# Two DMA queues for two streams of tiles: V loads issued from ScalarE, K loads from SyncE, in a cached attention decode kernel

## The chip, the cores and the metric

One core of one Trainium2 chip. The metric is the device time of the launch in microseconds (us), the median of several runs. Before the change: 2566.66 us (2565.97 to 2567.49, 3 runs). All runs that are compared are of the fast state, except where a line says otherwise.

Terms: PE is the matrix engine (TensorE), which also forms sums here by multiplying with an identity matrix; VectorE and ScalarE do the elementwise work; SyncE here only issues transfers. SBUF is the memory on the chip that tiles are loaded into. An engine *issues* a load into its own queue, the 16 DMA engines move it in packets, and it has *landed* when its completion records are in. PV is the product of the softmax weights with a V tile. "Page", "timeline" and "windows" are views of the profile of one execution.

## The reference, cut to what matters

```python
# twice, for A and for B; B=8 sequences, one new token each, H=32 heads, Sk=4096 keys, Dh=128, bf16
q = (x @ wq).reshape(B, 1, H, Dh).transpose(0, 2, 1, 3)
scores = einsum("bhqd,bhkd->bhqk", q, k_cache) * Dh ** -0.5
o = einsum("bhqk,bhkd->bhqd", softmax(scores), v_cache)
result = o.transpose(0, 2, 1, 3).reshape(B, 1, H * Dh) @ wo
```

The four caches are 1.07 GB, each byte used once. A decode step is one long read with a little arithmetic beside it.

## The kernel before

The work is cut into 64 steps, `n` (2 problems x 8 sequences x 4 groups of 8 heads). Each step needs one K tile and one V tile of 128 partitions x 64 KB (8.39 MB). The kernel keeps three in SBUF: K tiles alternate between slots 0 and 1, and all V tiles but the last share slot 2. So K is double-buffered and V is not. VectorE multiplies K with q and folds it, in four chunks; PE and VectorE finish the sums; the softmax weights are spread into `PM`; PE computes PV, in two halves.

```python
plan = [("wq", 0, 1), ("k", 0, 0), ("wq", 1, 2)]        # kind, number, slot
for n in range(NQ - 1):
    plan.append(("k", n + 1, (n + 1) % 2))
    plan.append(("v", n, 2))
...
def load_tiles():                       # issue what is next in the plan once its slot is free
    while issued[0] < len(plan):
        kind, n, w = plan[issued[0]]
        prev = before[issued[0]]        # the slot's former tenant
        dep = opUse.get(prev)           # its last reader on PE
        if prev is not None and dep is None:
            return
        to, key = ring[:, w, :], ("t", w)
        if kind in ("k", "v"):
            ...
            opT[(kind, n)] = dma(to, from_, key, [dep])     # SyncE's queue
...
for n in range(NQ):
    for r in range(NR):                 # NR = 4 chunks of a K tile
        make_mul(s)                     # VectorE, L330: waits for K
        if s >= LAG: make_red(s - LAG)  # VectorE, L353: waits for PE's sums of the chunk before
        ...
        fold = make_fold(s)             # VectorE, L335
        ...
        if r == 2 and n >= 1:
            make_pv(n - 1, 0, RG // 2)  # PE, L382: waits for V
        if r == 3 and n >= 1:
            make_pv(n - 1, RG // 2, RG)
            make_acc(n - 1)             # ScalarE: pv -> accS, L390
        if r == 2 and n + 1 < NQ: ...   # q of the next step (make_stage, make_qbc)
        make_eacc(s, fold)              # PE, L345: sums of this chunk; the fourth frees K's slot
        load_tiles()
        if r == 3 and n >= 1: make_ext(n - 1)   # PE, then ScalarE's small output copy
```

Note PE's order: the first half of PV stands ahead of chunk 2's sums. If V is late, PE waits, and VectorE soon waits behind PE.

Of the kernel before, what the change touches and what calls it, by code (L numbers as in the profile page):

```python
# [31 lines left out]
class _Program:  # L32
# [11 lines left out]
    def add(self, eng, emit, deps=(), dma_key=None, moves=False):  # L44
        op = _Op(eng, emit, list(deps), dma_key, moves)
        if dma_key is not None:
            self.counts[dma_key] = self.counts.get(dma_key, 0) + 16
            op.token = (dma_key, self.counts[dma_key])
        for d in op.deps:
            if not (d.eng == "pe" and eng == "pe"):  # L50
                d.sig = True
        self.ops[eng].append(op)
        return op
# [86 lines left out]
def _build_kernel(nc, caches, out):  # L140
    B, Sq, D = caches[0][0].shape
    _, H, Sk, Dh = caches[0][1].shape
    NC = len(caches)
    assert B == 8 and Sq == 1 and Dh == 128 and Sk == 4096 and D == 1024 and H % 8 == 0 and 128 % H == 0
# [7 lines left out]
    HB = H // HQ  # L152
    NQ = NC * HB * B
# [8 lines left out]
    with es:  # L162
# [19 lines left out]
        pe = sb("pe", [128, T], BF16)  # L182
# [17 lines left out]
        sems = {e: es.enter_context(nc.semaphore(f"c_{e}")) for e in ENGINES[1:]}  # L200
# [4 lines left out]
        P = _Program()  # L205
        add = P.add

        def dma(out_ap, in_ap, key, deps, eng="sp"):
            return add(eng, lambda e: e.dma_start(out_ap, in_ap), deps, dma_key=key)
# [21 lines left out]
        opT, opMul, opEacc, opRed, opNgm, opExp = {}, {}, {}, {}, {}, {}  # L231
# [18 lines left out]
        def where(n):  # L250

            return n // (B * HB), n // HB % B, n % HB
# [4 lines left out]
        def load_tiles():  # L257
            while issued[0] < len(plan):
                kind, n, w = plan[issued[0]]
                prev = before[issued[0]]  # L260
                dep = opUse.get(prev)
# [3 lines that stand above are left out]
                if kind in ("k", "v"):  # L265
                    c, b, hb = where(n)
                    from_ = caches[c][1 if kind == "k" else 2][b, hb * HQ:(hb + 1) * HQ].rearrange("u (m t) d -> (u m) (t d)", m=MP)
                    opT[(kind, n)] = dma(to, from_, key, [dep])
                elif kind == "wq":
                    opT[(kind, n)] = dma(to[:, 0:DC * H * Dh], caches[n][3].rearrange("(p k) n -> p (k n)", k=DC), key, [dep])  # L270
                else:
                    from_ = caches[n][4].rearrange("(p r) n -> p (r n)", r=H)
                    for i, (r0, r1) in enumerate(wo_cuts if n == NC - 1 else ((0, H),)):
                        opT[(kind, n, i)] = dma(to[:, r0 * D:r1 * D], from_[:, r0 * D:r1 * D], key if n < NC - 1 else ("w", i), [dep])
                issued[0] += 1
# [171 lines left out]
        def emit_xT(e):  # L447
# [5 lines left out]
            return i  # L453
        op_xT = opUse[("x", 0)] = add("pe", emit_xT, [c_ident, op_x[-1]])
        load_tiles()
        c_xT = add("dve", lambda e: e.tensor_copy(xT[:], misc_bf16[:, 0:NC * DC * B]), [op_xT])
        make_q(0)
# [5 lines left out]
        for n in range(NQ):  # L463
            P.mark(n)
            for r in range(NR):
                s = n * NR + r
                make_mul(s)
                if s >= LAG:
                    make_red(s - LAG)
                if r == LAG - 1 and n >= 1:  # L470
                    make_shift(n - 1)
                fold = make_fold(s)
                if r == LAG - 1 and n >= 1:
                    make_pm(n - 1)
                if n == 0 and r == 1:
                    for c in range(1, NC):
                        make_q(c)
                        make_qT(c)
                if r == 2 and n >= 1:
                    make_pv(n - 1, 0, RG // 2)  # L480
                if r == 3 and n >= 1:
                    make_pv(n - 1, RG // 2, RG)
                    make_acc(n - 1)
                if r == 2 and n + 1 < NQ:
                    make_stage(n + 1)
                    make_qbc(n + 1)
                make_eacc(s, fold)
                load_tiles()
                if r == 3 and n >= 1:
                    make_ext(n - 1)  # L490
        P.mark(NQ)
        n = NQ - 1
# [4 lines left out]
        make_pv(n, 0, RG)  # L497
        make_acc(n)
        load_tiles()
        make_ext(n)  # L500
        make_norm(1)
# [4 lines left out]
        counts = P.tokens()  # L506
        for o in op_x:
            o.token = (("x", 0), 16 * NC)
        loops = {"pe": (1, 2, (NQ - 2) // 2), "dve": (3, 2, (NQ - 4) // 2), "act": (3, HB, (NQ - 4) // HB)}

        @block.sync
        def _(eng):
            P.run("sp", eng, sems)
            eng.wait_ge(sems[("out", 0)], counts[("out", 0)])
# [4 lines left out]

        @block.scalar  # L520
        def _(eng):
            P.run("act", eng, sems, loops["act"])

        @block.vector
        def _(eng):
# [7 lines left out]
def bass_concat_heads__mha_block_cached__mha_block_cached__decode_kernel(  # L533
    nc, A_x, A_k_cache, A_v_cache, A_wq, A_wo, B_x, B_k_cache, B_v_cache, B_wq, B_wo, out,
):
    caches = [(A_x, A_k_cache, A_v_cache, A_wq, A_wo), (B_x, B_k_cache, B_v_cache, B_wq, B_wo)]
    _build_kernel(nc, caches, out)
# [28 lines left out]
```

## Time and profile before

| before | value | where |
|---|---|---|
| DMA engines' busy share, rate, steady state | 1.00, 433 GB/s | windows, 120 to 2400 us |
| bytes read | 1107.33 MB, 2557 us at that rate | page |
| VectorE busy per period of 38.7 us | 33.81 us | windows, 1013.5 to 1052.2 us |
| VectorE's wait for K | 303.4 us in all | page, L330 |

The page of the kernel before: span, busy time, DMA slices (a digit of 9 is 90% or more), the DMA queues (packets, MB, share of the 16 engines' time) and three groups of instructions (busy us, mean ns | idle us before, and what ended most of it): VectorE's L330, which waits for K, its L353, which waits for PE's sums, and PE's PV at L382:

```profile
span 2565.3 us, 18707 instructions
PE 1125.5 (44%) x7648; PEld 395.3 (15%) x7648; DVE 2172.4 (85%) x1043; ACT 130.0 (5%) x401; POOL 2.6 (0%) x14
...
DMA  9999999999999999999999999999999999999998
...
q1 hardware_dynamic: 19344, 1107.32, 99.8%
...
L330 DVE TENSOR_TENSOR ring<-ring,qbc 128x8192 bf16<-128x8192 bf16 x256 | 1131.1, 4418 | 303.4 <-DMA ring<-in_B_k_cache_dram 153.3
...
L353 DVE TENSOR_REDUCE s_sb<-red 128x64 f32<-128x1024 f32 x256 | 311.0, 1215 | 3.7 <-PE red L345 3.7
L382 PE MATMUL pv<-ring,PM 128*32 128x512 bf16 x4096 | 274.0, 415 | 4.6 <-DVE PM L370 4.6
...
ring<-in_A_k_cache_dram SPq DMA_DIRECT2D x32, 40.0
ring<-in_A_v_cache_dram SPq DMA_DIRECT2D x32, 27.9
```

VectorE is busy 85% of the time, but the DMA engines are busy all of it, in one queue. 1107.33 MB at 433 GB/s fill 2557 of the 2565 us: at this rate, by that estimate, no order of the same loads can win more than 0.4%.

The timeline before, cut to the issues, the PV halves and VectorE's starts on K (start us, us, engine, line, operation; in brackets the idle time before):

```profile
1002.91 1.91 PE L382 MATMUL pv<-ring,PM 128*32 128x512 bf16 x32
1004.86 0.33 SPq L209 DMA_DIRECT2D ring<-in_A_v_cache_dram  x1
...
1011.96 0.33 SPq L209 DMA_DIRECT2D ring<-in_A_k_cache_dram  x1
...
1013.51 4.42 DVE L330 TENSOR_TENSOR ring<-ring,qbc 128x8192 bf16<-128x8192 bf16 x1 [4.82 <-DMA ring<-in_A_k_cache_dram]
...
1035.51 1.91 PE L382 MATMUL pv<-ring,PM 128*32 128x512 bf16 x32
...
1041.64 1.91 PE L382 MATMUL pv<-ring,PM 128*32 128x512 bf16 x32
1043.60 0.33 SPq L209 DMA_DIRECT2D ring<-in_A_v_cache_dram  x1
```

Read it as turns. V is issued at 1004.9, as soon as PV has left its slot, but the engines are still on the K tile that VectorE receives at 1013.5. V flows after that, alone, for 19.35 us, and is there (27.9 us after its issue, 1032.8) before PE wants it at 1035.5. From then until its next issue at 1043.6 the V slot takes no data, and the engines spend that time on K. V's **turnaround**, landing to next issue, is hidden under K's turn.

### The profile page before, as it was taken

The page shows a single profiled execution, that of the slowest core. Times are in us where ns is not written, and L with a number is a line of the kernel's source. Part 1 is how long each engine was busy: PE and PEld are TensorE (multiplying, and loading weights), DVE is VectorE, ACT ScalarE, POOL GpSimd, SP SyncE. Part 2 cuts the span into 40 slices and gives each one's busy share as a digit, 9 for nine tenths or more (in the row PEclk, how much of TensorE's full clock was granted, in tenths as well). Part 3 has the DMA queues.
Part 4 walks back from the last instruction along what each step waited for, and adds up shares of the span by engine and source line. Part 5 has one row for each costly group of instructions (what it writes and reads, how often), then busy time and mean ns, then how long its engine had stood idle before and what let it go on. Part 6 is the DMA issues. An engine that isn't in the chain of part 4 may idle for free.

```text
span 2565.3 us, 18707 instructions
## 1 busy us (share of the span) xinstructions
PE 1125.5 (44%) x7648; PEld 395.3 (15%) x7648; DVE 2172.4 (85%) x1043; ACT 130.0 (5%) x401; POOL 2.6 (0%) x14
## 2 busy tenths in 40 slices
PE   2543443444444444444444434444444434434435
PEld 0111111111111111111111111111111111111112
DVE  2898898898898898898888888988988988988983
ACT  1100000000000000000000000000000000000000
POOL 0000000000000000000000000000000000000000
PEclk7666667676766767767766767667766757667677
DMA  9999999999999999999999999999999999999998
GB/s 425 425 425 441 433 433 433 433 435 431 435 431 435 431 435 432 435 431 435 432 435 431 435 431 436 430 436 430 437 429 437 429 437 430 436 431 435 431 436 381
DMA packets 19435, 1107.51 MB, mean 432 GB/s; under 512 B 2209, under 2 KB 2257, under 8 KB 2401
## 3 DMA queue, kind: packets, MB, share of 16 engines
q1 hardware_dynamic: 19344, 1107.32, 99.8%
q8 instruction: 7, 0.11, 0.0%
q10 hardware_dynamic: 80, 0.05, 0.0%
q14 instruction: 4, 0.02, 0.0%
HBM read 1107.33 MB, written 0.03 MB: 432 GB/s over the span
## 4 chain that ended last, share of the span: by engine, by line
DMA 51%; DVE 28%; issue 16%; PE 5%; another core or an unknown queue 0%; ACT 0%; DVEq 0%; SPq 0%
DMA ring<-in_B_k_cache_dram 25%; DMA ring<-in_A_k_cache_dram 25%; DVE ring L330 10%; DVE ring L335 10%; PE red L345 4%; DVE s_sb L353 4%; DVE PM L370 3%; DMA ring<-in_B_wo_dram 1%; DVE rmax L359 1%; DVE rtmp L360 0%; PE proj L433 0%; ACT PM L291 0%; PE o L285 0%; DVEq L135 0%
## 5 line engine op out<-in xcount | busy, mean ns | idle before, releaser
L345 PE MATMUL red<-ring,ident 128*128 128x512 bf16 x2048 | 785.6, 553 | 1380.5 <-DVE ring L335 1380.5
L330 DVE TENSOR_TENSOR ring<-ring,qbc 128x8192 bf16<-128x8192 bf16 x256 | 1131.1, 4418 | 303.4 <-DMA ring<-in_B_k_cache_dram 153.3
L335 DVE TENSOR_TENSOR ring<-ring 128x4096 bf16<-128x4096 bf16 x256 | 581.4, 2271 | 0.0
L345 PEld LDWEIGHTS red<-ring,ident 128*128 128x128 bf16 x2048 | 239.7, 128 | 1833.6 <-DVE ring L335 1482.9
L353 DVE TENSOR_REDUCE s_sb<-red 128x64 f32<-128x1024 f32 x256 | 311.0, 1215 | 3.7 <-PE red L345 3.7
L382 PE MATMUL pv<-ring,PM 128*32 128x512 bf16 x4096 | 274.0, 415 | 4.6 <-DVE PM L370 4.6
L370 DVE TENSOR_TENSOR PM<-pe,own_h 128x2048 bf16<-128x2048 bf16 x64 | 146.1, 2283 | 0.7 <-ACT pe L365 0.7
L382 PEld LDWEIGHTS pv<-ring,PM 128*32 128x32 bf16 x4096 | 103.9, 104 | 189.0 <-issue 116.3
L319 ACT ACTIVATE qbc<-misc 128x128 bf16<-128x128 f32 x64 | 17.8, 278 | 1072.4 <-PE misc L317 1072.4
L365 ACT ACTIVATE pe<-s_sb,ngm 128x256 bf16<-128x256 f32 x64 | 32.5, 508 | 468.5 <-DVE ngm L363 468.5
L390 ACT ACTIVATE accS<-pv 128x512 bf16<-128x512 f32 x64 | 38.2, 597 | 349.0 <-PE pv L382 349.0
L399 PEld LDWEIGHTS o<-accS,E 128*32 128x32 bf16 x1024 | 31.3, 100 | 49.4 <-issue 48.2
L399 PE MATMUL o<-accS,E 128*32 128x32 bf16 x1024 | 38.1, 185 | 0.7 <-ACT accS L390 0.7
L405 ACT ACTIVATE o_sb<-o 32x32 f32 (+1 forms) x64 | 11.9, 186 | 454.4 <-PE o L399 453.8
L305 DVE COPY qT<-misc 128x64 bf16<-128x64 bf16 x8 | 3.5, 435 | 33.3 <-PE misc L301 33.3
L359 DVE TENSOR_REDUCE rmax<-s_sb 128x1 f32<-128x256 f32 x64 | 26.9, 420 | 2.2
L438 DVE CAST orow<-proj 40x512 bf16<-40x512 f32 (+1 forms) x2 | 1.1, 554 | 26.7 <-PE proj L433 26.7
L433 PE MATMUL proj<-ring,on_sb 128*8 128x256 bf16 (+1 forms) x192 | 15.2, 395 | 13.8 <-DMA ring<-in_A_wo_dram 8.7
L312 ACT ACTIVATE qst<-qT 128x128 bf16 (+1 forms) x64 | 18.7, 293 | 2.0 <-DVE qT L305 2.0
L360 DVE TENSOR_SCALAR rtmp<-half,rmax 128x32 f32<-128x32 f32 x64 | 15.4, 241 | 2.2
L285 PE MATMUL o<-ring,xT 128*8 128x512 bf16 x64 | 7.1, 621 | 20.0 <-DMA ring<-in_A_wq_dram 11.0
L363 DVE TRANSPOSE_TENSOR_REDUCE ngm<-rtmp 128x1 f32<-128x32 f32 x64 | 13.5, 211 | 2.2
(33 smaller groups left out, 74.4 us busy)
## 6 DMA issues: line engine op xcount, KB each, us to landing
ring<-in_B_wo_dram SPq DMA_DIRECT2D x1, 6144.0 KB, 35.0
ring<-in_B_wo_dram SPq DMA_DIRECT2D x1, 1536.0 KB, 38.3
ring<-in_A_k_cache_dram SPq DMA_DIRECT2D x32, 40.0
ring<-in_A_v_cache_dram SPq DMA_DIRECT2D x32, 27.9
ring<-in_B_k_cache_dram SPq DMA_DIRECT2D x32, 39.8
ring<-in_B_v_cache_dram SPq DMA_DIRECT2D x32, 27.9
ring<-in_B_wo_dram SPq DMA_DIRECT2D x1, 512.0 KB, 39.0
out_dram<-orow SPq DMA_DIRECT2D x2, 4.0 KB
```

The lines of the kernel that those rows point to most:

```text
L312: return e.activation(qst[:, n % 2, :].rearrange("p (j m) -> p j m", m=MP), from_.unsqueeze(2).to_broadcast([128, HQ, MP]), ACTF.Copy)
L319: opQbc[n] = add("act", lambda e: e.activation(qbc[:, n % 2, :], misc[:, 0:Dh], ACTF.Copy), [opQb[n], _at(opMul, NR * (n - 2) + NR - 1)])
L330: opMul[s] = add("dve", lambda e: e.tensor_tensor(v, v, qbc[:, n % 2, :].unsqueeze(1).to_broadcast([128, CT, Dh]), ALU.mult), [opT[("k", n ...
L335: return add("dve", lambda e: e.tensor_tensor(v[:, :, 0:64], v[:, :, 0:64], v[:, :, 64:128], ALU.add), [opMul[s]])
L345: i = e.matmul(dst, ident[:], v[:, g, :, j, :], start=(j == 0), stop=(j == 3))
L353: opRed[s] = add("dve", lambda e: e.tensor_reduce(s_sb[:, n % 2, r * CT:(r + 1) * CT], red_ps[s % 2][:, :].rearrange("p (t w) -> p t w", w ...
L359: m = add("dve", lambda e: e.tensor_reduce(rmax[:], s_sb[:, n % 2, :], AX.X, ALU.max), [opRed[NR * n + NR - 1]])
L365: opExp[n] = add("act", lambda e, at: e.activation(pe[:], s_sb[:, n % 2, :], ACTF.Exp, bias=ngm[:, n % 2:n % 2 + 1], scale=scale, accum_ou ...
L370: opPM[n] = add("dve", lambda e: e.tensor_tensor(PM[:], pe[:].unsqueeze(2).to_broadcast([128, T, HQ]), own_h[:].unsqueeze(1).to_broadcast( ...
L382: i = e.matmul(pv_ps[32 * q:32 * (q + 1), :], PM[:, t:t + 4, :].rearrange("p t j -> p (t j)"), v[:, t * Dh:(t + 4) * Dh], start=(g == 0), ...
L390: opAcc[n] = add("act", lambda e: e.activation(accS[:], pv_ps[:], ACTF.Copy), [opPV[n], _at(opExt, n - 1)])
L399: x = e.matmul(to, E[:, i, PH - 1 - u:PH - 1 - u + MB], accS[:, i * 128 + H * u:i * 128 + H * (u + 1)], start=(i == 0 and u == 0), stop=(i ...
```

## The change

Its intent: do not hold a V load behind the K load that stands ahead of it in a queue; start it at once on a second queue. ScalarE then issues loads that can't stand in its loop, so its program is written out straight.

```diff
-                    opT[(kind, n)] = dma(to, from_, key, [dep])
+                    opT[(kind, n)] = dma(to, from_, key, [dep], "act" if kind == "v" else "sp")
...
-        loops = {"pe": ..., "dve": ..., "act": (3, HB, (NQ - 4) // HB)}
+        loops = {"pe": ..., "dve": ...}
...
-            P.run("act", eng, sems, loops["act"])
+            P.run("act", eng, sems)
```

More of the change, by code (lines that the diff above doesn't have):

```diff
@@ L508, in _build_kernel @@
             o.token = (("x", 0), 16 * NC)
-        loops = {"pe": (1, 2, (NQ - 2) // 2), "dve": (3, 2, (NQ - 4) // 2), "act": (3, HB, (NQ - 4) // HB)}
+        loops = {"pe": (1, 2, (NQ - 2) // 2), "dve": (3, 2, (NQ - 4) // 2)}
         @block.sync
```

## The prediction

> **What bounds the kernel now.** DMA. The page's slices show the 16 DMA engines 9 tenths busy or more; queue q1 is 99.8% of it. The kernel reads 1107.33 MB; in the steady state (windows view, 120 to 2400 us) the rate is 433 GB/s. All bytes at that rate take 2557 of 2565.3 us: under 0.5% is left to win. VectorE is next: 33.8 us busy per period of 38.7 us (one K and one V tile), with 4.8 us waiting for K (303.4 us in all, L330). One 8.39 MB tile takes 19.35 us.
>
> **Order now.** One queue serves whole tiles in turn. In the timeline V is issued at 1004.9, K at 1012.0, while the former K lands at 1013.5: V waits 8 us for its turn, then flows alone (27.9 us to landing). The 10 us in which PV holds the only V slot are covered by K's turn.
>
> **The change.** V gets a second queue. [...] ScalarE's second x load, 16 KB, issued at 1.4 us beside SyncE's loads, lands at 10.8. So V and K will share the rate half and half. Issue costs (0.3 to 0.6 us on ScalarE, 5% busy) and the straight ScalarE program cost nothing visible.
>
> **As a cycle.** Sharing stretches V, the tile with one slot. Let V land at t=0 with PE blocked on it (PV stands before chunk 2's reduction matmuls in PE's order, so VectorE blocks too):
> - PV half 3.4 [...], qbc 1, reduction 2.2, PV half 1.9, gaps 0.4: slot free at 8.9; accS copy 0.6; issue to first packet about 1: next V flows from 10.3.
> - VectorE: reduce 1.2, fold 2.3 end at 10.0; last reduction matmuls 1.9; next K issued at 12.0, flowing from 13.1.
> - V has 2 to 3 of its 8 packets per DMA engine (2.42 us each) alone, then alternates with K: 13 to 14 packet times, 31.4 to 33.9 us. It lands at 42 to 44.5; K two to three packets later, 5 to 7 us into the next cycle; then DMA idles until 10.3.
>
> VectorE wants V at 33 (22 us after its tile starts at 10.7), so it does wait and the cycle sustains itself. Period 42 to 45 instead of 38.7, all on the critical path: V's turnaround, hidden before. Today's phase leads there: sharing delays K's landing by 8 us, then V's issue. 63 periods of 43.6 plus the 128 us outside them (2565 - 63 x 38.7) give about 2880.
>
> **Prediction: 2880 us**, 8 in 10 within 2720 to 3060. Faster by over 2%: 0.01; within 2%: 0.10; slower by over 2%: 0.89.
>
> **What would show it.** Two queues, about half the bytes each; DMA busy near 0.9, about 385 GB/s; V's issue to landing up from 27.9 to about 33; PE waiting for V at L382 (about 10 us per period), VectorE's wait moving from L330 (K) to L353 (reduction); VectorE's busy time unchanged at 2172 us; period 42 to 45.
>
> **What would make it wrong.** If the DMA engines favour one queue, tiles keep landing one by one and the time stays near 2566. If K joins later or earlier than costed, the period moves by whole packets (2.4 us, 150 us in all). If PE's restart is quicker, the idle shrinks. If the phase locks so that V ends before it is wanted, the time is near the DMA bound again.

63 x 43.6 + 128 comes to 2875, about 2880. Two terms were estimates. Of the half share, the trace before shows only that the second queue is served while the first is busy: the two x loads' packets run from 1.8 to 10.1 us, while SyncE's wq load, issued at 0.81 us, takes 21.9 us to land. PV's 3.4 us has its likeness in the sums of 8 matmuls at L345: 3.60 us at 80.59 us, where TensorE's granted clock was 0.50 of full speed, and 1.90 us at 114.41 us, where it was 1.00.

## The result, and the profile after

After: 2931.91 us median (2924.83 to 2936.99, 3 runs), **14% slower**: ratio 1.1421, 95% interval 1.1401 to 1.1440. (Here and below a ratio is the mean time of one kernel's fast runs over that of the other's fast runs of the same rounds, so not quite the ratio of the medians.) The instructions of PE and VectorE are the same as before, in the same order.

The same lines of the page of the changed kernel, with a second queue:

```profile
span 2935.2 us, 18256 instructions
PE 1155.4 (39%) x7648; PEld 401.4 (14%) x7648; DVE 2172.8 (74%) x1043; ACT 130.0 (4%) x401; POOL 2.5 (0%) x14
...
DMA  9989889889889898898898898898988988988989
...
q1 hardware_dynamic: 10128, 570.45, 44.9%
q10 hardware_dynamic: 9296, 536.92, 43.7%
...
L330 DVE TENSOR_TENSOR ring<-ring,qbc 128x8192 bf16<-128x8192 bf16 x256 | 1131.4, 4420 | 13.6 <-DMA ring<-in_A_k_cache_dram 13.6
...
L353 DVE TENSOR_REDUCE s_sb<-red 128x64 f32<-128x1024 f32 x256 | 312.2, 1220 | 659.8 <-PE red L345 659.8
L382 PE MATMUL pv<-ring,PM 128*32 128x512 bf16 x4096 | 349.5, 502 | 799.9 <-DMA ring<-in_A_v_cache_dram 400.1
...
ring<-in_A_k_cache_dram SPq DMA_DIRECT2D x32, 37.6
ring<-in_A_v_cache_dram ACTq DMA_DIRECT2D x32, 36.3
```

Two queues carry half of the bytes each. The DMA engines are now busy 44.9 + 43.7 = 88.6% of the span instead of 99.8%. VectorE works as long as before, hardly waits for K (13.6 us) and waits 659.8 us behind PE, which waits 799.9 us for V. V takes 36.3 us from issue to landing instead of 27.9, although it is now first in its queue.

The chain of waits of the changed kernel between 1490 and 1560 us (start us, us, what):

```profile
1504.83 36.34 DMA ring<-in_B_v_cache_dram
1541.17 0.04 issue
1541.21 3.61 PE pv L382 x32
1544.82 0.22 PE misc L317
1545.04 2.28 PE red L345 x8
1547.32 1.87 PE pv L382 x32
1549.19 0.02 issue
1549.21 0.01 ACT accS L390
1549.21 38.88 DMA ring<-in_B_v_cache_dram
```

This is the whole period: V flows 36.34 us, PE needs 8.04 us to use it up, then the next V is issued; 1504.83 to 1549.21 is 44.38 us, against 38.7 before. The next one takes 38.88 us, one packet more. K appears nowhere: its issue lies beside this chain, as the timeline cut to SyncE (1490 to 1512 us) shows:

```profile
1508.38 0.33 SPq L209 DMA_DIRECT2D ring<-in_B_k_cache_dram  x1
```

So K joins 3.55 us after V. Each time the V slot is turned around, K has already ended: in the trace's packet records of this period the last K packet ends at 1545.6 and the next V packet starts at 1550.2. The 4.6 us between are idle on all 16 engines; 62 such stretches between the first tiles and the last sum to 293 us of the 370 us by which the span grew. Of the rest, 39 us is longer packets (their time per engine sums to 2600 us instead of 2561 us), and what is left, by subtraction, is time in which only some of the 16 are idle.

### The profile page after: what moved, and what is told of

It reads as the page before. It is cut to its first block, busy times and chain, and to the rows that moved or that the text cites. A ratio compares the mean times of both kernels' runs of the same rounds, so it can differ in the third digit from the quotient of the medians.

```text
span 2935.2 us, 18256 instructions
## 1 busy us (share of the span) xinstructions
PE 1155.4 (39%) x7648; PEld 401.4 (14%) x7648; DVE 2172.8 (74%) x1043; ACT 130.0 (4%) x401; POOL 2.5 (0%) x14
## 3 DMA queue, kind: packets, MB, share of 16 engines
q1 hardware_dynamic: 10128, 570.45, 44.9%
q10 hardware_dynamic: 9296, 536.92, 43.7%
HBM read 1107.33 MB, written 0.03 MB: 377 GB/s over the span
## 4 chain that ended last, share of the span: by engine, by line
DMA 79%; PE 17%; DVE 3%; another core or an unknown queue 0%; issue 0%; ACT 0%; SPq 0%; DVEq 0%
DMA ring<-in_A_v_cache_dram 39%; DMA ring<-in_B_v_cache_dram 37%; PE pv L382 11%; PE red L345 5%; DVE ring L330 1%; DMA ring<-in_A_k_cache_dram 1%; DMA ring<-in_B_wo_dram 1%; DVE ring L335 1%; PE misc L317 0%; DVE s_sb L353 0%; PE proj L433 0%; DVE PM L370 0%; PE o L285 0%; PE pv L285 0%
## 5 line engine op out<-in xcount | busy, mean ns | idle before, releaser
L330 DVE TENSOR_TENSOR ring<-ring,qbc 128x8192 bf16<-128x8192 bf16 x256 | 1131.4, 4420 | 13.6 <-DMA ring<-in_A_k_cache_dram 13.6
L345 PE MATMUL red<-ring,ident 128*128 128x512 bf16 x2048 | 746.2, 530 | 927.0 <-DVE ring L335 927.0
L353 DVE TENSOR_REDUCE s_sb<-red 128x64 f32<-128x1024 f32 x256 | 312.2, 1220 | 659.8 <-PE red L345 659.8
L382 PE MATMUL pv<-ring,PM 128*32 128x512 bf16 x4096 | 349.5, 502 | 799.9 <-DMA ring<-in_A_v_cache_dram 400.1
L345 PEld LDWEIGHTS red<-ring,ident 128*128 128x128 bf16 x2048 | 237.1, 125 | 1357.8 <-DVE ring L335 1023.8
L382 PEld LDWEIGHTS pv<-ring,PM 128*32 128x32 bf16 x4096 | 118.9, 117 | 1026.4 <-DMA ring<-in_A_v_cache_dram 427.6
L365 ACT ACTIVATE pe<-s_sb,ngm 128x256 bf16<-128x256 f32 x64 | 32.5, 508 | 257.4 <-DVE ngm L363 257.4
L399 PE MATMUL o<-accS,E 128*32 128x32 bf16 x1024 | 36.3, 177 | 0.7 <-ACT accS L390 0.7
L405 ACT ACTIVATE o_sb<-o 32x32 f32<-32x32 f32 x64 | 11.9, 186 | 226.6 <-PE o L399 226.0
L312 ACT ACTIVATE qst<-qT 128x128 bf16<-128x128 bf16 x64 | 18.7, 293 | 2.0 <-DVE qT L305 1.9
L317 PE MATMUL misc<-ident,qst 128*128 128x128 bf16 x64 | 18.2, 284 | 0.9 <-ACT qst L312 0.9
## 6 DMA issues: line engine op xcount, KB each, us to landing
ring<-in_A_k_cache_dram SPq DMA_DIRECT2D x32, 37.6
ring<-in_A_v_cache_dram ACTq DMA_DIRECT2D x32, 36.3
ring<-in_B_k_cache_dram SPq DMA_DIRECT2D x32, 37.6
ring<-in_B_v_cache_dram ACTq DMA_DIRECT2D x32, 36.3
```

What stands on the lines that cost most here:

```text
L312: return e.activation(qst[:, n % 2, :].rearrange("p (j m) -> p j m", m=MP), from_.unsqueeze(2).to_broadcast([128, HQ, MP]), ACTF.Copy)
L317: opQb[n] = add("pe", lambda e: e.matmul(misc[:, 0:Dh], qst[:, n % 2, :], ident[:], start=True, stop=True), [opSt[n], _at(opQbc, n - 1), c ...
L330: opMul[s] = add("dve", lambda e: e.tensor_tensor(v, v, qbc[:, n % 2, :].unsqueeze(1).to_broadcast([128, CT, Dh]), ALU.mult), [opT[("k", n ...
L345: i = e.matmul(dst, ident[:], v[:, g, :, j, :], start=(j == 0), stop=(j == 3))
L353: opRed[s] = add("dve", lambda e: e.tensor_reduce(s_sb[:, n % 2, r * CT:(r + 1) * CT], red_ps[s % 2][:, :].rearrange("p (t w) -> p t w", w ...
L365: opExp[n] = add("act", lambda e, at: e.activation(pe[:], s_sb[:, n % 2, :], ACTF.Exp, bias=ngm[:, n % 2:n % 2 + 1], scale=scale, accum_ou ...
```

## The experiments

The theory (**sharing**): the DMA engines alternate between the queues (measured under e8, e9, e11 below), so V and K divide the rate, V takes nearly twice as long, the single V slot becomes the critical path, and its turnaround, once under K's turn, lies open. The rivals: **A**, ScalarE's straight program costs; **B**, ScalarE or its queue is the worse one to load from; **C**, two queues at once make the engines less efficient. Each run gave a correct result. Edits are against the changed kernel.

| run | edit | us | ratio to before, 95% |
|---|---|---|---|
| after | the change | 2931.91 | 1.1421 (1.1401 to 1.1440) |
| e1_straight | V back to SyncE, ScalarE straight | 2566.51 | 0.9999 (0.9982 to 1.0016) |
| e2_all_act | K and V from ScalarE | 2574.81 | 1.0032 (1.0015 to 1.0049) |
| e3_swap | K from ScalarE, V from SyncE | 2931.47 | 1.1422 (1.1402 to 1.1443) |
| e4_split | each tile 64 + 64 partitions, two queues | 5026.45 | none (2 of 4 runs slow) |
| e5_k_after_exp | K issued about 5 us later | 2650.72 | 1.0364 (1.0304 to 1.0425) |
| e6_k_after_red | K issued after the next tile's first sums | 2578.40 | 1.0058 (1.0030 to 1.0086) |
| e7_v_after_ext | V issued 3.5 us later | 3421.02 | 1.3323 (1.3301 to 1.3346) |
| e8_k_small | K in packets of 32 KB | 2619.98 | 1.0209 (1.0192 to 1.0226) |
| e9_v_small | V in packets of 32 KB | 3188.40 | 1.2419 (1.2398 to 1.2439) |
| e10_v_halves | V freed, loaded, awaited by halves | 2578.31 | 1.0042 (1.0025 to 1.0059) |
| e11_both_small | K and V in packets of 32 KB | 2914.66 | 1.1351 (1.1333 to 1.1370) |
| e12_split_rows | each tile two half rows, two queues | 2585.52 | 1.0072 (1.0055 to 1.0089) |

### Which part of the change costs: e1, e2, e3, e4, e12

```diff
-  ... dma(to, from_, key, [dep], "act" if kind == "v" else "sp")
+  ... dma(to, from_, key, [dep], "sp")                              # e1
+  ... dma(to, from_, key, [dep], "act")                             # e2
+  ... dma(to, from_, key, [dep], "act" if kind == "k" else "sp")    # e3
```

> ScalarE's program straight as in the change, but all tiles issued from SyncE's queue. Sharing theory (V and K in two queues divide the DMA rate, V takes 36 us instead of 19, and the 10 us turnaround of its one slot is no longer covered): no second queue, so the time of before, 2566 us within 0.5%. Rival A (the straight ScalarE program costs): near 2930.

> K and V tiles and their order unchanged, but all of them issued from ScalarE's queue. Sharing theory: one queue, tiles land whole and in turn, 2566 to 2590 us. Rival B (ScalarE is the worse issuer, or its DMA queue the slower one): 2900 or more.

> The two queues exchanged: K from ScalarE, V from SyncE as soon as PV has left the slot. Sharing theory: the same sharing, so 2930 us (2890 to 2970), V's landing near 36 us. Rival B: V is back in SyncE's queue, so near 2570.

(In the first text 36 us is V's issue to landing and 19 us the flow alone; flow against flow it is 33 to 19.) e1 gave the time of before: the straight program costs nothing, and A falls. e2, with all K and V tiles from ScalarE, is 0.3% slower than before, and its trace has the landings of before (K 39.8 to 40.0 us, V 27.8) and 433 GB/s from 200 to 2400 us. e3, with the queues exchanged, is as slow as the change, V taking 36.3 to 36.4 us and K 37.6 to 37.7. In these runs it hardly matters which engine issues what (1.0032 for e2, 1.1422 for e3 against 1.1421); it matters that K and V stand in different queues. B falls.

Rival C needs both queues busy without K beside V. The first attempt cut each tile by partitions:

```diff
-  opT[(kind, n)] = dma(to, from_, key, [dep], "act" if kind == "v" else "sp")
+  dma(to[0:64], from_[0:64], key, [dep], "sp")
+  opT[(kind, n)] = dma(to[64:128], from_[64:128], key, [dep], "act")          # e4
```

> Every K and V tile is loaded as two DMAs of 64 partitions, one from each queue, in the order of before. Both queues are always in use at once, but no V shares with a K. Sharing theory: tiles land whole and in turn, 2566 to 2600 us. Rival C (two queues at once make the DMA engines less efficient): 2900 or more, with a lower rate while busy.

It came out at 5026 us, far from either number, and tells nothing about C, because the cut changed more than the queue: the DMA engines were busy all the time (share 1.00) and moved half as much (222 GB/s instead of 433). The windows view of this run (1000 to 4000 us; last two columns DMA share and GB/s):

```profile
1000.00:4000.00 3000.00, 682.70 (x4461) 237.19 (x4462) 1352.79 (x638) 73.64 (x238) 0.00 (x0) 0.59 1.00 222
```

Each 64 KB packet took about 4.84 us (median of the trace's packet records) instead of 2.42. It was not that one queue stood still while the other was served: their packets took 50.9% and 49.0% of the engines' time, and the packet records have both in flight at 99% of the instants from 1000 to 4000 us. What slowed the packets was not shown. The same question, cut by rows, so that every DMA reaches all 128 partitions:

```diff
-  opT[(kind, n)] = dma(to, from_, key, [dep], "act" if kind == "v" else "sp")
+  h = T * Dh // 2
+  dma(to[:, 0:h], from_[:, 0:h], key, [dep], "sp")
+  opT[(kind, n)] = dma(to[:, h:2 * h], from_[:, h:2 * h], key, [dep], "act")  # e12
```

> The question of the run e4_split, asked without its flaw (there each DMA reached only 64 partitions and each packet of 64 KB took 4.84 us instead of 2.42, so that the run told nothing of queues). Here every K and V tile is loaded as two DMAs of half rows over all 128 partitions, the first half from SyncE's queue, the second from ScalarE's, in the order of before: both queues are in use at once, but no V shares with a K. Sharing theory: tiles land whole and in turn, 32 KB packets take 1.21 us, 2566 to 2600 us. Rival C (two queues at once cost efficiency): 2900 or more, or packets slower than 1.21 us.

2585.52 us, as sharing had it; windows, e12:

```profile
200.00:2400.00 2200.00, 958.93 (x6363) 334.35 (x6360) 1911.33 (x907) 105.76 (x341) 0.00 (x0) 0.68 1.00 432
```

Two queues at once cost about 0.7% here, against the 14% of the change. The changed kernel itself says the same: while K and V flow side by side (the first queue view under e8, e9, e11 below), 3.15 + 3.15 MB in 14.5 us is 434 GB/s. C falls.

### A load that is issued later makes the kernel faster: e5, e6, e7

```diff
 dep = opUse.get(prev)
+if kind == "k" and n >= 2 and dep is not None: dep = opExp.get(n - 2)               # e5
+if kind == "k" and n >= 2 and dep is not None: dep = opEacc.get(NR * (n - 1))       # e6
+if kind == "v" and 1 <= n < NQ - 1 and dep is not None: dep = opExt.get(n - 1)      # e7
...
-  [dep], "act" ...
+  [dep, opUse.get(prev)], "act" ...
```

(In e7, `load_tiles()` is also called once more, after `make_ext`.)

> The changed kernel, but a K tile is issued 5 us later, after the next softmax exponential, though its slot is free before. Sharing theory: V has 8.6 us alone instead of 3.6, 11 to 12 packet times (2.42 us) instead of 14, and the period falls from 44.4 to 39 to 40 us: about 2620 us (2570 to 2700), faster than the changed kernel because a load is later. Rivals A to C: no gain, 2930 or more.

> The same with K issued 10 us later, after the next tile's first reduction matmuls. Sharing theory: V lands before or soon after K starts, so the tiles again go nearly in turn; 2590 us (2560 to 2650). VectorE's wait is for K again. Rivals A to C: 2930 or more.

> The changed kernel, but V is issued 4 us later, after the small output copy. Sharing theory: V starts 4 us later and also loses its time alone, so it takes 16 to 17 packet times instead of 14: period 52.7 to 55 us, about 3500 us (3400 to 3620). A rival in which only the turnaround is added to a fixed load time: 44.4 + 4.1, about 3190 us.

All three came inside their ranges. Nothing but a K load's issue was put off (in the runs' own timelines 5.5 us in e5 and 13.6 us in e6 after its slot was free), and 281 us (e5) and 354 us (e6) of the change's loss were gone. V's landing fell from 36.3 to 31.7 and to 27.8 us, the last being the value of before. In e7 V's issue after its landing came 3.5 us later than in the change (11.5 instead of 8.0 us in the critical chain), and V's issue to landing grew from 36.3 to 40.7 us, since K now starts ahead of V: 3.5 + 4.4 = 7.9 us a period, and 3421 - 2932 = 489 us is 7.8 us for each of 63 periods. V's delay is paid more than twice, while K's delay is earned. Windows of the three kernels, 200 to 2400 us, in this order: e5, e6, e7:

```profile
200.00:2400.00 2200.00, 948.75 (x6272) 330.33 (x6271) 1870.26 (x883) 103.11 (x332) 0.00 (x0) 0.67 0.98 421
```

```profile
200.00:2400.00 2200.00, 960.33 (x6402) 336.26 (x6401) 1919.97 (x910) 105.66 (x341) 0.00 (x0) 0.68 1.00 433
```

```profile
200.00:2400.00 2200.00, 717.25 (x4746) 250.63 (x4746) 1415.22 (x671) 78.13 (x252) 0.00 (x0) 0.64 0.75 319
```

The DMA share of 1.00 is back in e6, and VectorE's waits are those of before: 316.7 us for K at the multiply, 3.4 us behind PE.

### How the engines divide: e8, e9, e11

```diff
-  opT[(kind, n)] = dma(to, from_, key, [dep], "act" if kind == "v" else "sp")
+  if kind == "k":                       # e8; e9: if kind == "v"; e11: for both
+      h = T * Dh // 2
+      dma(to[:, 0:h], from_[:, 0:h], key, [dep], ...)
+      opT[(kind, n)] = dma(to[:, h:2 * h], from_[:, h:2 * h], key, [dep], ...)
+  else: ...
```

> The changed kernel, with each K tile loaded as two DMAs of half rows, so K's packets are 32 KB and V's 64 KB. Sharing theory with turns taken packet by packet: V gets two thirds of the rate, lands after about 11 packet times, the period is limited by the bytes again: 2590 us (2560 to 2680). If the engines share by bytes: unchanged, 2930.

> The changed kernel, with each V tile loaded as two DMAs of half rows, so V's packets are 32 KB and K's 64 KB. Sharing theory with turns packet by packet: V gets one third while K flows, lands after about 16 packet times of 2.42 us, period 49 us: 3225 us (3130 to 3320). Sharing by bytes: 2930.

> Control for the runs with half rows: the changed kernel with K and V both in two DMAs of half rows, whole tiles released and awaited as in the change. Sharing theory: an even share again, 2920 us (2860 to 2960), with fewer jumps of a whole packet. If small packets or more DMAs were what helped or hurt in the other runs, it differs by more.

The DMA queues (packets, MB, share) over 14.5 us in which V and K both flow; q1 is SyncE's with K, q10 ScalarE's with V. First the changed kernel (1514.5 to 1529 us), then e8 (the same window), then e9 (1500 to 1514.5 us):

```profile
q10 hardware_dynamic: 48, 3.15, 50.0%
q1 hardware_dynamic: 48, 3.15, 50.0%
```

```profile
q10 hardware_dynamic: 64, 4.19, 66.8%
q1 hardware_dynamic: 64, 2.10, 33.5%
```

```profile
q1 hardware_dynamic: 66, 4.33, 68.8%
q10 hardware_dynamic: 78, 2.03, 32.5%
```

The change and e8 have exactly as many packets in one queue as in the other, whatever their size; in e9 66 packets of K stand beside 62 of V and V's 16 completion records, which is even to within one turn of each engine. So turns were taken packet by packet here, and the queue with the larger packets got the larger share (66.8% to 33.5% in e8, 68.8% to 32.5% in e9). Give V two thirds and the kernel is nearly at the DMA bound again (2620 us); give it one third and it takes 3188 us; an even share in small packets is 0.6% from the change (2915). Halving a packet of K moves the time by -312 us, of V by +256 us, of both by -17 us: the size by itself does little, the share does.

### Shorten the turnaround and keep the sharing: e10

```diff
+first = opPVa.get(prev[1]) if kind == "v" and prev[0] == "v" else dep
+if kind == "v" and first is not None and ...:
+    halves.append(v_half(n, w, 0, first))      # first half row: freed by the first half of PV
...
+        halves.append(v_half(n, w, 1, dep))    # second: by the second half
...
-  op = add("pe", emit, [opPM[n], opT[("v", n)], ...
+  op = add("pe", emit, [opPM[n], opT[("v", n, 0)] if g0 == 0 else None, opT[("v", n, 1)] if g1 == RG else None, ...
```

(K too is loaded as two half rows, so that all packets are alike, as in e11.)

> All tiles in half rows (packets of 32 KB for both); each half of V has its own semaphore, is issued as soon as its half of PV has left, and is awaited by its half of PV. The two queues still share. Sharing theory: the first half of V flows from about 5.8 us after V's landing instead of 9.6, just when K ends, so DMA hardly idles: 2590 us (2560 to 2660). If sharing itself, not the uncovered turnaround, costs the time: 2900 or more.

2578.31 us, though K and V are in two queues and still share: in the packet records each queue has 40 to 60% of the bytes in 46% of the stretches of 4.84 us (in the change 62%). Compare e11, 2914.66 us, which has packets of the same size and the same queues but treats V as a whole. Windows, e10, then the queues of e11's page:

```profile
200.00:2400.00 2200.00, 969.75 (x6364) 336.86 (x6365) 1913.88 (x908) 105.20 (x340) 0.00 (x0) 0.68 1.00 432
```

```profile
q1 hardware_dynamic: 19344, 570.45, 45.3%
q10 hardware_dynamic: 18512, 536.93, 43.9%
```

In e10 the engines are busy all the time, in e11 89.2% of it. So sharing by itself is not the loss. The loss here is that a single-buffered tile that is stretched by sharing leaves the engines nothing to do while it is turned around (4.6 us in the period shown). With V in halves the next data come before K has run out.

No version beat the kernel before; e1 equals it, e2 stays 8 us over it, and e6 and e10 11 us. By the estimate from the page before (1107.33 MB at 433 GB/s) none could by more than 0.4%.

## Why the prediction was right, point by point

- *Bound.* DMA at 99.8% in the page before, with under 0.5% to win. e2, e6, e10 and e12, four other ways of ordering the same bytes, all run at 432 to 433 GB/s in their middles and end within 0.8% of it.
- *Sharing half and half.* An estimate when it was made; the trace after shows it: 48 packets to 48. That a second queue would bring no bandwidth was read from the page before (99.8%), and with both queues flowing the rate was 434 GB/s against 433; that it hurts by 14% does not follow from the page, and needed the cycle.
- *Restart of PE, slot free after 8.9 us, accS 0.6, issue about 1: next V flows at 10.3.* The chain measured 8.04 us from V's landing to the next issue (PV 3.61 at a granted clock of 0.50, where the half at 1035.51 us in the timeline before, without the wait, takes 1.91 at 1.00; qbc 0.22, sums 2.28, PV 1.87, gaps), and the accS copy does not hold up the issue at all: both start at 1549.21. The first packet came 1.0 us after the issue, so 9.0 us.
- *V flows 13 to 14 packet times, 31.4 to 33.9 us.* This is the term that was mis-sized. V's issue to landing was 36.3 us where about 33 was predicted. The trace's packet records of the tile issued at 1504.83 show three V packets before K's first turn, then five pairs of K and V: 13 packet times, as costed, and the last V data end at 1538.4. But the completion records come at 1540.1 to 1540.8, each when one more K packet has ended. That is the fourteenth packet time. (Whether they wait for a turn of their queue or for that packet's writes, the records do not tell.) The first packet after the idle stretch also took 3.1 us instead of 2.42.
- *Period 42 to 45 us.* 44.4 us in most periods. In the packet records, 6 of the 56 periods looked at are 46.7 to 47.1: one packet more, as foreseen under "the period moves by whole packets". The two errors, restart too long and flow too short, partly cancel, so 2880 against 2932: that it came so near is in part luck; the mechanism is not.
- *What would show it.* DMA share near 0.9 (0.886), about 385 GB/s (377), V at L382 about 10 us per period (799.9 / 64 = 12.5, more than foreseen), VectorE's wait moved from L330 (303.4 to 13.6 us) to L353 (3.7 to 659.8 us), VectorE's busy time unchanged (2172.8 us): all seen. K's landing comes out of the cycle as costed at 35 to 39.5 us after its issue (42 + 5 - 12 to 44.5 + 7 - 12); it was 37.6.
- *ScalarE's straight program costs nothing.* e1: 0.9999.

Open: why e4's packets took about twice as long, why each engine's first 64 KB packet after an idle stretch takes 3.1 us, and why K's first packet came 5.1 us after its issue in the period shown (V's 1.0 us), which gave V three packets alone.

## What to carry to other kernels

In this kernel, where DMA is the bound, one queue is a schedule: it delivered whole tiles one after the other, and the tile in its turn got the full rate (8.39 MB in 19.35 us, 433 GB/s). A second queue turned that into sharing, so that a tile flows for longer (V for 33 us instead of 19), and the buffer with the fewest slots was the one exposed. In another kernel, look for the time in which it takes no data, and ask what the DMA engines will do meanwhile. If two queues are needed, two remedies worked here: to free and load the scarce buffer in pieces (e10, 2578 us), or to hold back the other stream (e6, 2578 us). In e6 the later load was the faster one: 2578 us against 2932.
